# The gates' rows made on TensorE instead of through DRAM, column sums as one-column products, and a warm-up of three long products, in an adaLN block with linear attention

## The chip, the cores and the metric

One core of one Trainium2 chip. The metric is the device time of one execution of the program in microseconds (us); a lower one is better. The engines are called PE (TensorE, with PEld for its weight loads), DVE (VectorE), ACT (ScalarE), POOL (GpSimd) and SP (SyncE, which issues most transfers). Each engine works through its own instructions in the order in which the program has them, and waits on semaphores for the others.

## What is computed

A transformer block on x of 2048 tokens x 640 channels, with 32 heads of 20 channels. A vector c gives six modulation rows of 640 values; two of them, `ga` and `gb`, are the gates.

```python
mod = (_silu(c) @ w_mod).reshape(c.shape[0], 6, 1, -1)
sa, ca, ga, sb, cb, gb = (mod[:, 0], ..., mod[:, 5])
h = _layernorm(x) * (1 + ca) + sa
x = x + ga * A(h)          # linear attention, then @ wo
h = _layernorm(x) * (1 + cb) + sb
x = x + gb * B(h)          # relu(h @ w1 + b1)**2 @ w2 + b2
```

In the attention q and k go through a per-head matrix `w_phi` and two softmaxes each (of the product and of its negative); `kv` is the sum over tokens of phi_k times v, `z` the sum of phi_k, and the output is phi_q kv / (phi_q z + 1e-6). All inputs are float32.

## The kernel before

The weights of k and q are first folded with `w_phi` on TensorE (`fold`, L276). Then the 2048 tokens are worked in 16 tiles of 128. Nearly every large product is made of three: each operand is split into a high part (rounded to the fast float32r form by a ScalarE copy) and a low part (the rest, a VectorE subtraction, `lo`, L91 to L92), and high x high, high x low and low x high are added up in PSUM (`three`, `mm`).

The program has these stages. Up to about 60 us: warm-up products, the folds, the first tiles. From 60 to about 210 us: a loop over t = 2 to 13. In it TensorE's order is written by hand; the other engines' instructions are placed by a list scheduler, held only by some `issue_after` marks. Each turn makes the k, v and q products of a tile (`proj`, L82), and at even t the K/V sums of two tiles (`do_kv`, L453: 32 fp32 products a tile, each of two records, in four groups of 32 columns of the array), which gather in the PSUM bank `kvp[0]`. From 210 us a section ordered by hand on every engine but SP: the last tiles, the last K/V sums, the copy `kvs` of their bank to SBUF (ACT, L795), the row sums `z` spread over the partitions (`make_z`, PE L818, copied to `zb` by ACT L829 and DVE L827/L831), and then, tile by tile, the attention's output: DVE multiplies stored exponents by `zb` and sums them (L880, L882), makes the tails `ut` (L905) and the scaled exponents `ezb` (L916), which TensorE transposes (`tail` L932, `te` L950) and multiplies by K/V; then the product with `wo`. From about 376 us the MLP.

The modulation rows that are needed late (parts 2 to 5: `ga`, `sb`, `cb`, `gb`) are made beside this. For each part, DVE multiplies five row blocks of `w_mod` by the column `cs` = silu(c) and adds them up (`mac`, L290 and L292) into one tile of 128 x 640, called `wm` in the trace. What is still missing is the sum over the 128 partitions. Before the change it is made thus (`mod_turn` and `mod_sum`): PE transposes the tile in five blocks of 128 (L302; four after the K/V sums at t = 6, 8, 10 for parts 2, 3, 4, the fifth in the next turn's `t1`; all five in `kv_diags` for part 5), ACT copies the transposes to `mt` (L303), and DVE sums along the free axis (L307). That gives a column of five values on each partition. For parts 3 and 4 the column is what is wanted (`cols_b`, shift and scale of the second norm; 1 is added to the scale at t = 12). The gates are needed as a row on every partition: the column `gate_a` is written to DRAM, 4 bytes at a time, and read back to all partitions as `ga_b` (`spread_row`, SP L325 and L326, in t = 7). `ga_b` multiplies the rows of `wo` (`prep_wo`, from t = 9). The column `gate_b` is transposed on PE (L1284), copied by ACT (L1285), written to DRAM and read back as `gb_b` (SP L1286, L1287) when the attention ends; `gb_b` is used at the MLP's output.

The multiplies of part 5 (`gb_mac`) stand in the ordered section, the last two of them just before `biases`, the last two `do_kv` and the copy `kvs`.

The warm-up (L621, L623) is nine fp32 products of `ones` with `ones`, 128 x 128, and seven of 1 x 1; an fp32 product leaves two records.

Of the kernel before, what the change touches and what calls it, by code (L numbers as in the profile page):

```python
# [22 lines left out]
NC = D // P  # L23
# [8 lines left out]
CUT = ((0, 384), (384, D))  # L32
V_HEADS = ((0, 19), (19, H - 1))
EPS = 1e-5
POSTPONED = 4
WARM = 9
SHORT = 7
KEPT = NT - POSTPONED
W2_AT = 48
PLAIN = 2  # L40
# [15 lines left out]
def kernel(  # L56
# [23 lines left out]
    def mm(o, terms, first=True, last=True, skip=False):  # L80
        for i, (a, b) in enumerate(terms):
            nc.tensor.matmul(  # L82
                o, a, b,
                start=first and i == 0, stop=last and i == len(terms) - 1,
                skip_group_check=skip,
            )
# [4 lines left out]
    def lo(out_lo, full, hi, eng=None):  # L91
        (eng or nc.vector).tensor_tensor(out_lo, full, hi.bitcast(F32), op=ALU.subtract)  # L92
# [28 lines left out]
    def row(tag, name):  # L121
        return (pc if tag in ("s3", "s4") else mem).tile([P, D], F32, tag=tag, name=name, bufs=BUFS[tag])
# [19 lines left out]
    def tp(name):  # L142
        return psA.tile([P, 512], F32, tag="tp", name=name)
# [20 lines left out]
    ident = const.tile([P, P], F32, name="ident")  # L164
    make_identity(nc, ident)
    neg = const.tile([P, P], F32R, name="neg")
    plus = const.tile([P, 1], F32, name="plus")
    nc.gpsimd.memset(plus, 0.0)
    nc.gpsimd.memset(plus[32:64], 1.0)
# [90 lines left out]
    nc.vector.tensor_tensor(cs, c_t, ce, op=ALU.mult)  # L260

    nc.scalar.activation(neg, ident, AF.Copy, scale=-1.0)

    W = {}

# [25 lines left out]
        else:  # L291
            nc.vector.scalar_tensor_tensor(acc, t, cs[:, k : k + 1], prev, op0=ALU.mult, op1=ALU.add)  # L292

    MT = {}

    def mod_turn(part, p, *cs_):
        t = MT.setdefault(part, None) or row("s1", f"mt{part}")
        MT[part] = t
        a, n = cs_[0] * P, len(cs_) * P
        for i, c in enumerate(cs_):  # L300
            src = by_turn(MA[part])[:, c] if part in (3, 4) else MA[part][:, c * P : (c + 1) * P]
            nc.tensor.transpose(p[:, i * P : (i + 1) * P], src, ident)  # L302
        nc.scalar.activation(t[:, a : a + n], p[:, :n], AF.Copy)  # L303

    def mod_sum(part, dest):
        with tc.issue_after(newest(ET_.DVE)):
            nc.vector.tensor_reduce(dest, MT[part].rearrange("p (a b) -> p a b", b=P), axis=AX.X, op=ALU.add)  # L307

    def stage(col, k):
        t = row("s1", f"wm{col}_{k}")  # L310
# [11 lines left out]
    GD = [dram.tile([NC, P], F32, name=f"gate{h}") for h in range(2)]  # L322

    def spread_row(h, col, dest):
        nc.sync.dma_start(GD[h].rearrange("c p -> p c"), col)  # L325
        nc.sync.dma_start(dest, GD[h].rearrange("c p -> (c p)")[None, :].to_broadcast([P, D]))  # L326

    def ln_parts(xt, nm, spare=None):
        sm = small([P, 2], "sm", f"sm{nm}")
# [22 lines left out]
    def by_turn(ap):  # L352
        return ap.rearrange("p (f b) -> p b f", b=NC)
# [29 lines left out]
    def t1(j, *ds, more=None):  # L383
# [5 lines left out]
        if more:  # L389
            mod_turn(more[0], p[:, 256:], 4)  # L390
# [3 lines left out]
        if more:  # L394
            mod_sum(*more)

    def proj(nm, t, *between, cut=CUT):
        p = pj(f"p{nm}{t}")
# [60 lines left out]
    def do_q(t, *between):  # L459
        q_out(t, proj("q", t, *between))  # L460
# [42 lines left out]
    def biases():  # L503
        nc.sync.dma_start(bb, bass.AP(tensor=b2.tensor, offset=b2.offset, ap=[[0, P], [1, D]]))
# [7 lines left out]
    def gb_mac(n=1):  # L512
        for _ in range(n):
            k, t = GB.pop(0)
            mac(t, t, k, MA.get(5))
            MA[5] = t

    def wo_weights(*gs):
        for g in gs:
            prep_wo(g, ga_b)  # L520

    AFTER_KV = {
        6: lambda: mod_turn(2, tp("mc2"), 0, 1, 2, 3),
        8: lambda: mod_turn(3, tp("mc3"), 0, 1, 2, 3),
        10: lambda: mod_turn(4, tp("mc4"), 0, 1, 2, 3),
        12: lambda: t1(NT // 2 - 1, 2, 3),
    }
    gate_a = const.tile([P, NC], F32, name="gate_a")
    gate_b = const.tile([P, NC], F32, name="gate_b")
    gate_r = pc.tile([NC, P], F32, name="gate_r")  # L530
    LAST_COL = {7: (2, gate_a), 9: (3, cols_b[:, 0:5]), 11: (4, cols_b[:, 5:10])}
    SIDE = {
        2: lambda: mod_mac(2, 0, 1, 2),
        3: lambda: (mod_mac(2, 3, 4), mod_mac(3, 0)),
        4: lambda: mod_mac(3, 1, 2),
        5: lambda: (mod_mac(3, 3, 4), mod_mac(4, 0)),
        6: lambda: mod_mac(4, 1, 2),
        7: lambda: (spread_row(0, gate_a, ga_b), mod_mac(4, 3)),
        8: lambda: mod_mac(4, 4),
        9: lambda: wo_weights(0, 1),  # L540
        10: lambda: wo_weights(2),
        11: lambda: None,
        12: lambda: (nc.vector.tensor_scalar(cols_b[:, 5:10], cols_b[:, 5:10], 1.0, None, op0=ALU.add), wo_weights(3, 4)),
        13: lambda: gb_load(),
    }

# [71 lines left out]

    warm = tp("warm")
    for i in range(WARM):  # L620
        nc.tensor.matmul(warm[:, :P], ones, ones, start=True, stop=True)  # L621
    for i in range(SHORT):
        nc.tensor.matmul(warm[:1, :1], ones[:, :1], ones[:, :1], start=True, stop=True)  # L623
    for d in range(4):
        fold("k", d)()
    n0 = stats(XB[0], "a0")
# [84 lines left out]
    for t in range(2, NT - 2):  # L711
        j, i = divmod(t, 2)
        if i == 0 and j < NT // 2 - 2:
            load_x(j + 2)
        PK[t] = row("s2", f"k{t}")
        to_sb(proj("k", t), PK[t])
        if t == NT - 4:
            t1(j + 1, 0, 1)
        norm = j + 1 if i == 0 and t < NT - 4 else j + 2 if t == NT - 5 else None
        if norm:  # L720
            if not i:
                parts = ln_parts(XB[norm], f"a{norm}")
# [12 lines left out]
        spread(PK[t], EK[t], f"k{t}")  # L735
        exps(EK[t])
        if norm and not i:
            next(parts)
        if i and t < NT - 4:
            t1(j + 1, 2, 3)  # L740
        with tc.issue_after(newest(ET_.DVE)):
            k_norm(EK[t], t)
        if t < NT - POSTPONED:
            do_q(t, *([(1, 3, lambda: t1(j + 1, 4, more=LAST_COL.get(t)))] if i else []))
            if norm and i:
                with tc.issue_after(newest(ET_.Activation)), tc.issue_after(DONE[0]):
                    next(parts)
            if i:
                with tc.issue_after(DONE[1]):
                    q_chain(t)  # L750
            else:
                q_chain(t)
        if i == 0 and t < NT - 4:
            t1(j + 1, 0, 1)
        if t == NT - 6:
            parts = ln_parts(XB[j + 2], f"a{j + 2}")
            with tc.issue_after(newest(ET_.Activation)):
                next(parts)
        SIDE[t]()
# [28 lines left out]
    exps(EQ[q0])  # L788
    q_sums(q0)
    gb_mac(2)  # L790
    biases()
    do_kv(ka)
    do_kv(kb)
# [6 lines left out]
    def bank(nm):  # L800
        return psB.tile([P, 512], F32, tag="m", name=nm)
# [413 lines left out]
    for j in range(NB):  # L1215
# [16 lines left out]
            e_prod(b)  # L1232
        e_recip(b - 1)
        e_scale(b - 1)
        if j == 6:
            mod_sum(5, gate_b)
        load_e(b + 2)
        do_wo(j, 0, 0, *hooks(0, 0))
        if j - 1 in SPREAD:
# [559 lines left out]
```

## Time and profile before

| what | value |
|---|---|
| timed runs, median of 3 | 747.1 us (746.55 to 747.64) |
| the profiled execution's own time | 746.04 us |
| its span | 744.3 us |
| PE busy | 736.7 us (99%) |
| DVE busy | 599.0 us (80%) |
| ACT busy | 454.4 us (61%) |
| POOL busy | 168.1 us (23%) |
| granted clock, mean | 1.0 |

The profiled execution is one run, and its time is 1.74 us more than its span. In the rows of the profile, "L302 PE MATMUL mc<-ident,wm ... x4" is a group of four instructions of line 302 on PE that write `mc` and read `ident` and `wm`. A timeline's row begins with start and duration, and a bracket at its end gives the idle time of the engine before it and what ended that. A waits row gives total, number and longest wait.

### The profile page before, as it was taken

The numbers are of one execution on the slowest core, as the hardware profiler recorded it, in microseconds if no ns is written. First come the engines' busy times: TensorE is split into PE (matmuls) and PEld (weight loads), VectorE is DVE, ScalarE is ACT, GpSimd is POOL, SyncE is SP. The second block draws the span as 40 slices with busy tenths as digits, with TensorE's granted clock in tenths as the row PEclk, the third lists the DMA queues.
The fourth block names the chain that finished last, engine by engine and source line by source line (L and its number), as shares of the span: only waits on it lengthen the run. The fifth ranks groups of instructions, "written<-read, shape, count | busy, mean of one in ns | idle before, by whom it ended". The sixth has DMA issues, their size and how long they took to land.

```text
span 744.3 us, 16676 instructions
## 1 busy us (share of the span) xinstructions
PE 736.7 (99%) x6537; PEld 718.8 (97%) x6537; DVE 599.0 (80%) x1089; ACT 454.4 (61%) x1060; POOL 168.1 (23%) x352
## 2 busy tenths in 40 slices
PE   9999999999999999999999999999999999999997
PEld 9999999999999889998999999999999999999997
DVE  6598988978999999999655777877786776777766
ACT  5767666667863365567687667475573747647431
POOL 2001101001000347647303040231321313222110
PEclk9999999999999999999999999999999999999999
DMA  9912341343432354754885567897667768667461
GB/s 325 344 37 107 120 129 56 107 142 108 139 111 72 99 168 167 166 129 107 210 249 169 151 198 260 272 312 210 185 187 200 211 183 241 185 177 215 129 183 36
DMA packets 58801, 126.47 MB, mean 170 GB/s; under 512 B 7438, under 2 KB 16403, under 8 KB 58723
## 3 DMA queue, kind: packets, MB, share of 16 engines
q1 hardware_dynamic: 38636, 79.20, 32.6%
q0 software_dynamic: 17504, 40.90, 21.8%
q10 hardware_dynamic: 2583, 5.30, 1.9%
q8 instruction: 51, 0.84, 0.5%
q14 instruction: 27, 0.22, 0.1%
HBM read 100.74 MB, written 29.89 MB: 176 GB/s over the span
## 4 chain that ended last, share of the span: by engine, by line
PE 83%; DVE 10%; ACT 3%; issue 2%; POOL 1%; DMA 1%; ACTq 0%; DVEq 0%; POOLq 0%
PE up L82 25%; PE acc L82 18%; PE pwo L82 8%; PE pk L82 7%; PE pv L82 5%; PE acc3x L82 5%; PE pq L82 5%; PE te L950 2%; DVE dn L882 1%; DVE sk L444 1%; PE foldk L276 1%; PE numa L82 1%; DVE ek L436 1%; DVE ek L446 1%; DVE scr L880 1%
## 5 line engine op out<-in xcount | busy, mean ns | idle before, releaser
L82 PE MATMUL up<-h,w 128*128 128x256 f32 x1640 | 204.6, 276 | 0.1
L82 PEld LDWEIGHTS up<-h,w 128*128 128x128 f32 x1640 | 196.4, 188 | 0.7 <-DVE h L92 0.5
L1345 ACT ACTIVATE ft<-up,b_t 128x256 f32<-128x256 f32 x104 | 48.9, 471 | 95.7 <-PE up L82 95.3
L82 PE MATMUL acc<-w,ra 128*128 128x384 f32 x452 | 97.4, 335 | 0.0
L1346 DVE TENSOR_TENSOR ft<-ft 128x256 f32<-128x256 f32 x104 | 44.3, 426 | 42.9 <-ACT ft L1345 41.5
L82 PE MATMUL pwo<-wo,ot 128*128 128x384 f32 (+1 forms) x480 | 78.5, 314 | 0.0
L82 PE MATMUL pq<-wq,hT 128*128 128x384 f32 (+1 forms) x480 | 75.6, 312 | 0.0
L82 PEld LDWEIGHTS acc<-w,ra 128*128 128x128 f32 x452 | 72.7, 188 | 0.9 <-DVE ra L92 0.6
L82 PE MATMUL pk<-wk,hT 128*128 128x384 f32 (+1 forms) x480 | 73.1, 309 | 0.1
L82 PEld LDWEIGHTS pwo<-wo,ot 128*128 128x128 f32 x480 | 69.8, 188 | 2.8 <-issue 2.7
L82 PEld LDWEIGHTS pq<-wq,hT 128*128 128x128 f32 x480 | 71.1, 188 | 0.7 <-issue 0.5
L82 PE MATMUL pv<-wv,hT 128*128 128x384 f32 (+1 forms) x480 | 71.7, 307 | 0.0
L82 PEld LDWEIGHTS pk<-wk,hT 128*128 128x128 f32 x480 | 70.4, 188 | 1.0 <-DVE hT L92 0.5
L82 PEld LDWEIGHTS pv<-wv,hT 128*128 128x128 f32 x480 | 70.1, 188 | 0.0
L92 DVE TENSOR_TENSOR ra<-ft,ra 128x384 fp32r<-128x384 f32 (+2 forms) x86 | 36.8, 449 | 32.6 <-ACT ra L1369 18.8
L1455 POOL DMA_DIRECT2D ring_a<-td_a x34 | 18.5, 543 | 117.3 <-PE acc L82 106.3
L1369 ACT ACTIVATE ra<-ft 128x384 fp32r<-128x384 f32 x48 | 25.2, 526 | 28.4 <-DVE ft L1346 22.4
L82 PE MATMUL acc3x<-w,ra 128*128 128x256 f32 x231 | 39.5, 277 | 0.0
L82 PEld LDWEIGHTS acc3x<-w,ra 128*128 128x128 f32 x231 | 37.2, 188 | 0.0
L444 DVE TENSOR_REDUCE sk<-ek 128x64 f32<-128x1280 f32 x16 | 23.7, 1482 | 14.6 <-ACT ek L439 10.1
L1360 DVE TENSOR_TENSOR ft<-ft 128x128 f32<-128x128 f32 x136 | 33.4, 287 | 1.2
L335 POOL TENSOR_SCALAR sma<-sma 128x2 f32<-128x2 f32 x6 | 2.1, 343 | 133.7 <-ACT xb L334 133.7
(258 smaller groups left out, 1448.7 us busy)
## 6 DMA issues: line engine op xcount, KB each, us to landing
ring_c<-td_c POOLq DMA_DIRECT2D x34, 384.0 KB, 3.9
ring_a<-td_a POOLq DMA_DIRECT2D x34, 384.0 KB, 3.4
ring_b<-td_b POOLq DMA_DIRECT2D x34, 256.0 KB, 3.5
esp<-eq SPq DMA_DIRECT2D x12, 640.0 KB
el<-esp SPq DMA_DIRECT2D x12, 640.0 KB
rw<-in_w SPq DMA_DIRECT2D x23, 320.0 KB
wm<-in_w_mod SPq DMA_DIRECT2D x20, 320.0 KB
xb<-in_x SPq DMA_DIRECT2D x8, 640.0 KB
```

The lines of the kernel that those rows point to most:

```text
L82: nc.tensor.matmul(o, a, b, start=first and i == 0, stop=last and i == len(terms) - 1, skip_group_check=skip,)
L92: (eng or nc.vector).tensor_tensor(out_lo, full, hi.bitcast(F32), op=ALU.subtract)
L276: nc.tensor.matmul(p[g // 3][:, (g % 3) * 120 : (g % 3) * 120 + n], r, bd_t[:120, g * 120 : g * 120 + n], start=True, stop=True,)
L436: nc.vector.tensor_tensor(heads(e[:, s]), heads(t), over(mx[:, s]), op=ALU.subtract)
L444: nc.vector.tensor_reduce(s, heads(flat(e)), axis=AX.X, op=ALU.add)
L446: nc.vector.tensor_tensor(heads(flat(e)), heads(flat(e)), over(s), op=ALU.mult)
L950: nc.tensor.transpose(p[:124, a : a + P], EU[2 * j + i][:, 2 * g + c, :124], ident)
L1345: nc.scalar.activation(r, p, AF.Relu, bias=b1_t[:, f : f + 1])
L1346: nc.vector.tensor_tensor(r, r, r, op=ALU.mult)
L1360: nc.vector.tensor_tensor(t[:, o], t[:, a], t[:, b], op=op)
L1369: nc.scalar.activation(a[:, 0, :3], t[:, :3], AF.Copy)
L1455: nc.gpsimd.dma_start(RING[j, n, r], TD[n][r].bitcast(F32R))
```

## The change

It does four things.

1. Warm-up: three products of 128 x 384 columns (`ones` read three times) in place of nine of 128 and seven of one column.
2. Gates (parts 2 and 5): `gate_parts` splits the tile of 128 x 640 into a high part (ACT, L307 of the new kernel) and a low part (DVE, L91). `gate_row` multiplies a 128 x 128 matrix of ones (`ones_r`) by both, so that every partition of PSUM holds the sum over partitions, and ACT copies the row to `ga_b` or `gb_b` (L315). For part 2 the parts are made in t = 4 and the row at t = 6 in the place of the transposes (two products of 384 columns and two of 256); for part 5 the parts stand right behind the last two `gb_mac`, and the row is made in `kv_diags` (two products of 128 columns, two of 512). The DRAM tiles, their four transfers, the transpose L1284 and the copy L1285 are gone.
3. Parts 3 and 4: `mod_col` makes the column by 20 one-column fp32 products each (32 strided columns of the tile as the stationary operand, one column of ones moving, round four column groups), at t = 8 and 10 in the place of the transposes. ACT's copy adds the 1 to part 4. `mod_sum` is gone.
4. The fifth transposes of t = 7, 9, 11 (`more=`) are gone.

```diff
-WARM = 9
-SHORT = 7
+WARM = 3
...
+    nc.scalar.activation(ones_r, ones, AF.Copy)
...
-    def mod_turn(part, p, *cs_):
...
-    def mod_sum(part, dest):
...
+    def mod_col(part, dest):
+        m, p = by_turn(MA[part]), kvp[1]
+        for d in range(NC):
+            for c in range(0, P, 32):
+                nc.tensor.matmul(p[c : c + 32, d : d + 1], m[:, d, c : c + 32], ones[:, :1], start=(d == 0), stop=True, skip_group_check=True)
+        nc.scalar.activation(dest, p[:, :NC], AF.Identity, bias=ones[:, :1] if part == 4 else 0.0)
+
+    def gate_parts(part):
+        with tc.issue_after(newest(ET_.Activation)), tc.issue_after(newest(ET_.DVE)):
+            hi, low = GR_[part] = [row("s1", f"gate{part}_{i}").bitcast(F32R) for i in range(2)]
+            nc.scalar.activation(hi, MA[part], AF.Copy)
+            lo(low, MA[part], hi)
+
+    def gate_row(part, dest, *banks):
+        r = ones_r
+        for (a, b), p in banks:
+            mm(p, [(r, g[:, a:b]) for g in GR_[part]], skip=True)
+        for (a, b), p in banks:
+            nc.scalar.activation(dest[:, a:b], p, AF.Copy)
...
-    def spread_row(h, col, dest):
-        nc.sync.dma_start(GD[h].rearrange("c p -> p c"), col)
-        nc.sync.dma_start(dest, GD[h].rearrange("c p -> (c p)")[None, :].to_broadcast([P, D]))
...
-        6: lambda: mod_turn(2, tp("mc2"), 0, 1, 2, 3),
-        8: lambda: mod_turn(3, tp("mc3"), 0, 1, 2, 3),
-        10: lambda: mod_turn(4, tp("mc4"), 0, 1, 2, 3),
+        6: lambda: gate_row(2, ga_b, (CUT[0], kvp[1][:, :384]), (CUT[1], kvp[2][:, :256])),
+        8: lambda: mod_col(3, cols_b[:, 0:5]),
+        10: lambda: mod_col(4, cols_b[:, 5:10]),
...
-    LAST_COL = {7: (2, gate_a), 9: (3, cols_b[:, 0:5]), 11: (4, cols_b[:, 5:10])}
...
-        4: lambda: mod_mac(3, 1, 2),
+        4: lambda: (gate_parts(2), mod_mac(3, 1, 2)),
...
-        7: lambda: (spread_row(0, gate_a, ga_b), mod_mac(4, 3)),
+        7: lambda: mod_mac(4, 3),
...
     for i in range(WARM):
-        nc.tensor.matmul(warm[:, :P], ones, ones, start=True, stop=True)
-    for i in range(SHORT):
-        nc.tensor.matmul(warm[:1, :1], ones[:, :1], ones[:, :1], start=True, stop=True)
+        nc.tensor.matmul(warm[:, : 3 * P].rearrange("p (a n) -> p a n", a=3), ones, ones[:, None, :].to_broadcast([P, 3, P]), start=True, stop=True)
...
     gb_mac(2)
+    gate_parts(5)
     biases()
     do_kv(ka)
     do_kv(kb)
...
-        mod_turn(5, kvt[0][:, 3 * P :], 4)
-        mod_turn(5, bank("mc5"), 0, 1, 2, 3)
+        gate_row(5, gb_b, ((4 * P, D), kvt[0][:, 3 * P :]), ((0, 4 * P), bank("mc5")))
...
-            p = tp("gbt")[:NC, :P]
-            nc.tensor.transpose(p, gate_b, ident)
-            nc.scalar.activation(gate_r, p, AF.Copy)
-            nc.sync.dma_start(GD[1], gate_r)
-            nc.sync.dma_start(gb_b, GD[1].rearrange("c p -> (c p)")[None, :].to_broadcast([P, D]))
```

Two places show how the instructions now stand. The first is ACT at the end of the K/V sums (about 245 us before): `eq` are the exponents of tile 12, `wm_4` the finished tile of part 5, `gate_0` its high part, `kvs` the copy of the K/V bank, `zb` the copies of z. Before:

```order
L424 ACTIVATE vt_105<-pv_1_3324 128x16
L439 ACTIVATE eq_3083<-eq_3083 128x640
L440 ACTIVATE eq_3083<-eq_3083 128x640
L795 ACTIVATE kvs<-kvp_76 128x360
L829 ACTIVATE zb<-z_3450 128x3x60
L829 ACTIVATE zb<-z_3452 128x3x60
```

And in the changed kernel:

```order
L422 ACTIVATE vt_106<-pv_1_3329 128x16
L437 ACTIVATE eq_3088<-eq_3088 128x640
L438 ACTIVATE eq_3088<-eq_3088 128x640
L307 ACTIVATE gate_0_3369<-wm_4_3082 128x640
L790 ACTIVATE kvs<-kvp_76 128x360
L824 ACTIVATE zb<-z_3459 128x3x60
L824 ACTIVATE zb<-z_3461 128x3x60
```

A copy that needs the fifth multiply of part 5 now stands between the exponents and the copy `kvs`. On DVE that fifth multiply stands after the sum `rs_q` of the same exponents, and the low part behind it.

The second place is PE after the K/V sums at t = 8, where `mc` was the bank of part 3's transposes and `kvp_77` is the second K/V bank. Before:

```order
L82 MATMUL pv_1_2023<-wv_587,hT_1803 128x256 x3
L453 MATMUL kvp_76<-ek_1744,vt_104 21x2x20 x32
L453 MATMUL kvp_76<-ek_1894,vt_105 21x2x20 x32
L302 MATMUL mc_2118<-ident,wm_4_1580 128x128 x4
L82 MATMUL pq_0_2150<-wq_321,hT_1803 128x384 x3
```

And in the changed kernel:

```order
L81 MATMUL pv_1_2007<-wv_573,hT_1792 128x256 x3
L451 MATMUL kvp_76<-ek_1733,vt_105 21x2x20 x32
L451 MATMUL kvp_76<-ek_1883,vt_106 21x2x20 x32
L299 MATMUL kvp_77<-ones,wm_4_1570 32x1 x20
L81 MATMUL pq_0_2148<-wq_307,hT_1792 128x384 x3
```

Four transposes give way to 20 one-column products; what stands around them is the same. At t = 6 the four transposes give way to the gate row's four products in the same way.

More of the change, by code (lines that the diff above doesn't have):

```diff
@@ L166 @@
     neg = const.tile([P, P], F32R, name="neg")
+    ones_r = const.tile([P, P], F32R, name="ones_r")
     plus = const.tile([P, 1], F32, name="plus")
@@ L292, in mac @@
             nc.vector.scalar_tensor_tensor(acc, t, cs[:, k : k + 1], prev, op0=ALU.mult, op1=ALU.add)
-    MT = {}
-    def mod_turn(part, p, *cs_):
[L297 to L303, printed above, removed]
-    def mod_sum(part, dest):
-        with tc.issue_after(newest(ET_.DVE)):
-            nc.vector.tensor_reduce(dest, MT[part].rearrange("p (a b) -> p a b", b=P), axis=AX.X, op=ALU.add)
+    def mod_col(part, dest):
[4 more added lines that the diff above has]
+        nc.scalar.activation(dest, p[:, :NC], AF.Identity, bias=ones[:, :1] if part == 4 else 0.0)
+    GR_ = {}
+    def gate_parts(part):
[9 more added lines that the diff above has]
+            nc.scalar.activation(dest[:, a:b], p, AF.Copy)
     def stage(col, k):
@@ L320, in mod_mac @@
             MA[part] = t
-    GD = [dram.tile([NC, P], F32, name=f"gate{h}") for h in range(2)]
-    def spread_row(h, col, dest):
-        nc.sync.dma_start(GD[h].rearrange("c p -> p c"), col)
-        nc.sync.dma_start(dest, GD[h].rearrange("c p -> (c p)")[None, :].to_broadcast([P, D]))
     def ln_parts(xt, nm, spare=None):
@@ L381, with t1 @@
     DONE = []
-    def t1(j, *ds, more=None):
+    def t1(j, *ds):
         if 0 in ds:
@@ L388, in t1 @@
             t_in(XB[j], d, p[:, 256 * k : 256 * k + 256])
-        if more:
-            mod_turn(more[0], p[:, 256:], 4)
         for k, d in enumerate(ds):
@@ L393, in t1 @@
         DONE[:] = newest(ET_.Activation), newest(ET_.DVE)
-        if more:
-            mod_sum(*more)
     def proj(nm, t, *between, cut=CUT):
@@ L522 @@
     AFTER_KV = {
-        6: lambda: mod_turn(2, tp("mc2"), 0, 1, 2, 3),
-        8: lambda: mod_turn(3, tp("mc3"), 0, 1, 2, 3),
-        10: lambda: mod_turn(4, tp("mc4"), 0, 1, 2, 3),
+        6: lambda: gate_row(2, ga_b, (CUT[0], kvp[1][:, :384]), (CUT[1], kvp[2][:, :256])),
+        8: lambda: mod_col(3, cols_b[:, 0:5]),
+        10: lambda: mod_col(4, cols_b[:, 5:10]),
         12: lambda: t1(NT // 2 - 1, 2, 3),
     }
-    gate_a = const.tile([P, NC], F32, name="gate_a")
-    gate_b = const.tile([P, NC], F32, name="gate_b")
-    gate_r = pc.tile([NC, P], F32, name="gate_r")
-    LAST_COL = {7: (2, gate_a), 9: (3, cols_b[:, 0:5]), 11: (4, cols_b[:, 5:10])}
+    const.tile([P, 2 * NC], F32, name="fill3")
+    pc.tile([P, P], F32, name="gap4")
     SIDE = {
@@ L542 @@
         11: lambda: None,
-        12: lambda: (nc.vector.tensor_scalar(cols_b[:, 5:10], cols_b[:, 5:10], 1.0, None, op0=ALU.add), wo_weights(3, 4)),
+        12: lambda: wo_weights(3, 4),
         13: lambda: gb_load(),
@@ L743 @@
         if t < NT - POSTPONED:
-            do_q(t, *([(1, 3, lambda: t1(j + 1, 4, more=LAST_COL.get(t)))] if i else []))
+            do_q(t, *([(1, 3, lambda: t1(j + 1, 4))] if i else []))
             if norm and i:
@@ L1234 @@
         e_scale(b - 1)
-        if j == 6:
-            mod_sum(5, gate_b)
         load_e(b + 2)
```

## Prediction

> **What bounds the kernel now.** I read the page's busy times first, then TensorE's waits, then the timeline around each edit.
>
> ```profile
> span 744.3 us, 16676 instructions
> PE 736.7 (99%) x6537; PEld 718.8 (97%) x6537; DVE 599.0 (80%) x1089; ACT 454.4 (61%) x1060; POOL 168.1 (23%) x352
> ```
>
> TensorE (PE) is busy for 736.7 of 744.3 us, so an edit counts by the TensorE time that it removes or adds, or by a wait of TensorE that it makes or ends. The next view names TensorE's waits between 245 and 345 us, the attention stage.
>
> ```profile
> PE tail L932 <- DVE ut L905: 0.8, 2, 0.7
> PE tail L932 <- DVE ot L92: 0.6, 1, 0.6
> ```
>
> TensorE waits 1.4 us there, always for VectorE (DVE). How near VectorE is to its own limit is in the windows of 20 us (time, then busy time of PE, PEld, DVE, ACT, POOL):
>
> ```profile
> 245.00:265.00 20.00, 19.32 (x146) 17.60 (x147) 19.06 (x25) 8.26 (x23) 6.33 (x12) 1.00 0.51 159
> 325.00:345.00 20.00, 19.42 (x149) 17.79 (x148) 19.45 (x24) 13.93 (x33) 10.87 (x26) 1.00 0.52 141
> ```
>
> VectorE is busy for 19.06 and 19.45 of 20 us: in this stage both engines are nearly full, and a delay of either can reach the end. The granted clock is 1.00 in both.
>
> **Part 1, the warm-up.** TensorE's and VectorE's first rows (start, duration):
>
> ```profile
> 1.05 3.80 PE L621 MATMUL warm<-ones 128*128 128x128 f32 x18 [1.05 <-POOL bdc L159]
> 4.78 0.49 PE L623 MATMUL warm<-ones 128*1 128x1 f32 x14
> 5.20 1.04 PE L276 MATMUL foldk<-bd_t,raw_k 120*128 120x120 f32 x7
> 4.31 0.85 DVE L244 TENSOR_TENSOR bd_t<-bdc 120x360 f32<-120x360 f32 x2 [2.05 <-POOL mask L190]
> ```
>
> The new three products of 384 columns pass as many columns as nine of 128, so I let them end where the old nine end. The 14 short records between 4.78 and 5.20 fall away. The first fold then waits for the first of the two L244 instructions, which ends about half of 0.85 us after 4.31, with some overlap: 4.8 to 4.9. Gain 0.3 us; bounds 0 (a later load sets the folds) and 0.4.
>
> **Part 2, the column sums at t = 6, 8, 10.** Here are the K/V block and what follows it, without transposes (60 us), for part 2 (118 us) and part 4 (180 us).
>
> ```profile
> 60.37 1.48 PE L453 MATMUL kvp<-ek,vt 128*21 128x40 f32 x128
> 61.77 1.13 PE L82 MATMUL pq<-wq,hT 128*128 128x384 f32 x5
> ...
> 117.97 1.48 PE L453 MATMUL kvp<-ek,vt 128*21 128x40 f32 x128
> 119.38 0.66 PE L302 MATMUL mc<-ident,wm 128*128 128x128 f32 x4
> 119.79 1.48 PE L82 MATMUL pq<-wq,hT 128*128 128x384 f32 x7
> ...
> 178.83 1.48 PE L453 MATMUL kvp<-ek,vt 128*21 128x40 f32 x128
> 180.24 0.73 PE L302 MATMUL mc<-ident,wm 128*128 128x128 f32 x4
> 180.73 1.49 PE L82 MATMUL pq<-wq,hT 128*128 128x384 f32 x7
> ```
>
> From the block's start to the next product is 1.40 us without transposes, 1.82 and 1.90 with: four cost 0.42 and 0.50, and part 3 (rows below) 0.49. Together 1.41. The fifth transposes at t = 7, 9, 11, at a quarter of that each, add 0.36. What comes in their place has no row of its own, so it is priced by the nearest ones:
>
> ```profile
> L82 PE MATMUL pq<-wq,hT 128*128 128x384 f32 x167 | 32.3, 343 | 0.0
> L82 PE MATMUL pq<-wq,hT 128*128 128x256 f32 x165 | 22.1, 281 | 0.0
> L453 PE MATMUL kvp<-ek,vt 128*21 128x40 f32 x1024 | 12.6, 204 | 1.0 <-issue 0.9
> ```
>
> The gate's row at t = 6 is two products of 384 columns (32.3 / 167 = 0.193 us each) and two of 256 (0.134): 0.65. A column sum is 20 fp32 products, of two records each. Like the K/V products of L453 (12.6 / 1024 = 12.3 ns a record), they go round four column groups: 40 x 12.3 ns = 0.49 us, 0.98 for both. The other end is L623 above, 14 one-column records in one column group from 4.78 to 5.20, 30 ns each: 2.4 for both. I take 0.98, since L453 shares the column groups. Sum: -1.41 - 0.36 + 0.65 + 0.98 = -0.14.
>
> The Trainium skill, "TensorE: Matmul & The Clock Gate", section "Wait — 56ns, not 53.3ns?", says that start-to-start never falls below about 25 ns, however few columns pass. By that rule the 80 records would take 2.0 us and the sum would be 1.0 worse; L453's 12.3 ns speak against it.
>
> One more wait goes, that of the next transposes for ScalarE's (ACT's) copy of the sums:
>
> ```profile
> 124.72 0.66 PE L358 MATMUL ta<-ident,xb 128*128 128x128 f32 x4 [0.31 <-ACT mt L303]
> ```
>
> That is -0.3. The other copies, the VectorE sums of L307 and the gate's column turned at t = 7 of the output stage show in no wait of TensorE; I cost them, the two new VectorE subtractions of part 2 and the list scheduler's new order of loads and vector work before 210 us at nothing, 0.3 either way.
>
> **Part 3, the gate's write through DRAM.** The next rows are TensorE's and then SyncE's at t = 8, and after them the instruction queue's share of 16 DMA engines in 147 to 150.2 us and in 127 to 133 us.
>
> ```profile
> 147.87 1.50 PE L453 MATMUL kvp<-ek,vt 128*21 128x40 f32 x83
> 150.30 0.72 PE L453 MATMUL kvp<-ek,vt 128*21 128x40 f32 x45 [0.92 <-issue]
> 150.95 0.73 PE L302 MATMUL mc<-ident,wm 128*128 128x128 f32 x4
> 151.44 0.42 PE L82 MATMUL pq<-wq,hT 128*128 128x384 f32 x1
> ...
> 141.40 0.38 SPq L325 DMA_DIRECT2D gate<-gate_a  x1
> 150.25 0.34 SPq L326 DMA_DIRECT2D ga_b<-gate  x1
> ```
> ```profile
> q8 instruction: 1, 0.02, 6.1%
> ```
> ```profile
> q8 instruction: 1, 0.02, 0.9%
> ```
>
> This K/V block takes 150.95 - 147.87 = 3.08 us where another takes 1.41, and no semaphore is named. One instruction packet takes 6.1% of 16 x 3.2 = 3.1 us, against 0.9% of 16 x 6 = 0.9 in the other window. The gate's write of 4-byte values, issued at 141.40, is waited for until 150.25, just when TensorE goes on. I read it as an instruction fetch held up with that write. The change removes the write: -1.67 us. The other end is 0.
>
> The Trainium skill, "Runtime: NRT & Kernel Launch", section "Instruction fetch mechanics", says that crossing a 16 KiB block of instructions is mostly hidden. By that rule nothing comes back here and the time is 1.67 longer; this trace shows one crossing that is not hidden.
>
> **Part 4, the second gate's parts ahead of the K/V copy.** In the new order ScalarE's copy `gate_0` (L307) stands just before the copy `kvs`, and it needs the fifth multiply of the gate (L292). The rows before, ScalarE, VectorE and TensorE:
>
> ```profile
> 244.73 0.72 ACT L440 ACTIVATE eq<-eq 128x640 f32<-128x640 f32 x1
> 245.35 0.46 ACT L795 ACTIVATE kvs<-kvp 128x360 f32<-128x360 f32 x1
> 247.37 0.86 ACT L829 ACTIVATE zb<-z 128x180 f32<-128x180 f32 x4 [1.56 <-PE z L818]
> ...
> 246.88 1.80 DVE L292 SCALAR_TENSOR_TENSOR wm<-wm,cs,wm 128x640 f32<-128x640 f32 x2
> 249.44 0.28 DVE L827 COPY zb<-z 128x120 f32<-128x120 f32 x1
> 249.75 1.49 DVE L880 TENSOR_TENSOR scr<-el,zb 128x1280 f32<-128x1280 f32 x1
> ...
> 246.46 0.87 PE L818 MATMUL z<-kvs,ident 21*128 21x360 f32 x8
> ```
>
> The multiplies end at 248.68. A copy of 128x640, priced by the exponent's 0.72, ends at 249.4; `kvs`, 0.46 more, at 249.85. TensorE's z products, which ran at 246.46, wait on `kvs`: 3.4 us late, with the whole in-order queue of TensorE behind them. VectorE's side: ScalarE copied z from 0.91 us after z's start to 1.77 after it, so now until 251.6, and VectorE's last copy of z (0.28) lets L880 start at about 252.0 instead of 249.75: 2.25 late. The new subtraction on VectorE, priced by a multiply's 0.9, starts at 249.4 and lies inside that wait.
>
> Behind it stands the gate's row, in the place of five transposes:
>
> ```profile
> 253.04 0.27 PE L302 MATMUL kvt<-ident,wm 128*128 128x128 f32 x1
> 253.51 0.72 PE L82 MATMUL pq<-wq,hT 128*128 128x256 f32 x4
> L982 PE MATMUL numa<-ot,neg 128*128 128x512 f32 x2 | 0.9, 447 | 0.0
> ```
>
> The five took 0.47. Two products of 128 columns (0.11 each, as the transposes) and two of 512 (0.26 by the 384-column row's rate, 0.45 by L982) make 0.74 to 1.12: +0.3, bounds 0.2 and 0.65.
>
> So TensorE comes 3.4 + 0.3 = 3.7 late, and gives back the 1.4 that it used to wait for VectorE: 2.3 remain. VectorE is 2.25 late and full, so it cannot give much back, and where it paced TensorE (340 us) that is the same 2.3. Taken: +2.3; bounds 2.0 and 3.0.
>
> **Sum.** -0.3 - 0.14 - 0.3 - 1.67 + 2.3 = -0.1 us. The profiled execution took 746.04 us (span 744.3 and 1.74 around it), so it would take 745.9. The three timed runs of before have a median 1.06 above it, 747.1; on their scale I predict 747.0: gains before 160 us that the wait at 246 us takes back.
>
> **The rivals.**
>
> *The late fetch is not the gate's doing* (slower, 14%). For it: the row names only "issue", and timed and profiled runs differ by 1.06 us, so the profile may hold an accident. Against it: both ended together. If any fetch may come late in the dense K/V block, nothing is gained: 748.7. It decides once less than 0.2 of the 1.67 comes back.
>
> *Column products at 30 ns a record* (11%). For it: L623's rate, and strided weights. Against: L453. 1.4 more: 748.4.
>
> *The long warm-up does not open the clock in time* (8%). The clock is then low while the folds run; the old loop's records took 3.80 / 18 = 0.21 us, the old folds' 1.04 / 7 = 0.15, and if a stretch as long as the warm-up's 3.8 us ran at half speed, 1.9 would be lost, less what loads hide: about 1.7 more, 748.7. Against it: the same columns in the same time.
>
> *The timed runs hold more of the late fetch than the profiled one* (faster, 22%). Their surplus of 1.06 us would then go too: 745.9, and between 744.9 and 746.4 with the bounds of the other terms. For it: only a cause outside the profiled run explains the surplus. Against it: nothing shows where it lies.
>
> *The change does not do what it says*: the z wait would fail to appear only if ScalarE reached `gate_0` with the multiplies long done; they end 3.3 us after `kvs` started before, so I give this no chance of its own.
>
> **How the numbers follow.** 45% stay with the forecast, 747.0, whose own range is 746.0 to 748.4 (column products dear at the top; z's delay 2.0 and the gains at their best below). About 0.2%, 1.5 us, is what a measurement of this kernel tells from no change: faster means under 745.6, slower over 748.6. Of the forecast's 45%, 9 are faster, 31 the same, 5 slower; of the fetch rival's 14%, 9 slower and 5 the same; of the column rival's 11%, 7 the same and 4 slower; of the clock's 8%, 6 slower and 2 the same; of the surplus's 22%, 15 faster and 7 the same. Sums: 0.24, 0.52, 0.24. The range that leaves out 2 in 10 is 744.8 to 749.2.
>
> **What would show it.** In the changed kernel's profile: first fold near 4.9; no wait of `ta` for ScalarE at 124; K/V block at t = 8 of 1.4 us and no instruction packet of 3 us; column sums of 0.5 us each; a wait of TensorE of about 3.4 us at z, released by `kvs`, and none for VectorE at the next tail. A z wait under 2 us, or TensorE's waits for VectorE still there after it, would make part 4 wrong; a K/V block still at 3 us, part 3.

## The result, and the profile after

The changed kernel takes 754.53 us (median of 4, 752.78 to 755.70), the kernel before beside it 747.37. The ratio is 1.0085, with a 95% interval of 1.0064 to 1.0106: slower by about 6.4 us (the two medians are 7.2 apart), where no change was forecast and 749.2 was the range's upper end. The profiled execution took 752.78 us, 6.74 more than that of before. One timed run below, of the kernel with the column sums apart, took 1227 us at a mean granted clock of 0.558 and is left out of its ratio.

The page's first lines, and TensorE's longest waits in the changed kernel:

```profile
span 751.1 us, 16752 instructions
PE 739.1 (98%) x6578; PEld 719.6 (96%) x6578; DVE 598.4 (80%) x1086; ACT 454.5 (61%) x1060; POOL 171.9 (23%) x352
...
PE z L813 <- ACT kvs L790: 3.1, 1, 3.1
PE kvp L299 <- issue: 2.2, 1, 2.2
...
PE acc L81 <- DMA ring_b<-td_b: 0.6, 1, 0.6
PE tail L926 <- POOL rn L1150: 0.4, 1, 0.4
```

The span grew by 6.8 us and TensorE's busy time by 2.4, so 4.4 of the loss is time in which TensorE stands still. Two long waits are new: one for `kvs` ahead of z, one named only "issue" in the column products. The waits for VectorE at the tails are gone; one of 0.4 us for GpSimd (`rn`) came there, and one of 0.6 us for a transfer in the MLP.

Around z, the rows of ScalarE, TensorE and VectorE in the changed kernel, and last TensorE's rows before the change (z itself, at 246.46, is shown above):

```profile
249.13 0.74 ACT L307 ACTIVATE gate<-wm 128x640 fp32r<-128x640 f32 x1 [3.27 <-DVE wm L293]
249.77 0.45 ACT L790 ACTIVATE kvs<-kvp 128x360 f32<-128x360 f32 x1
...
245.28 1.85 PE L81 MATMUL pq<-wq,hT 128*128 128x384 f32 x9
250.28 1.57 PE L813 MATMUL z<-kvs,ident 21*128 21x360 f32 x8 [3.14 <-ACT kvs L790]
251.77 7.95 PE L81 MATMUL pq<-wq,hT 128*128 128x384 f32 x36
259.56 0.49 PE L835 MATMUL kvt<-ident,kvs 128*120 128x128 f32 x3
260.58 1.64 PE L81 MATMUL pq<-wq,hT 128*128 128x256 f32 x13
...
253.39 1.49 DVE L874 TENSOR_TENSOR scr<-el,zb 128x1280 f32<-128x1280 f32 x1
```
```profile
244.71 1.82 PE L82 MATMUL pq<-wq,hT 128*128 128x384 f32 x9
...
247.27 5.61 PE L82 MATMUL pq<-wq,hT 128*128 128x384 f32 x36
252.72 0.49 PE L840 MATMUL kvt<-ident,kvs 128*120 128x128 f32 x3
```

ScalarE waits 3.27 us for the fifth multiply, copies the gate's high part, and only then `kvs`. From the first q product to z it is 5.00 us here and 1.75 before: 3.25 more, as the prediction had it (3.4). But then the 36 q products from z's end to the turned K/V take 259.56 - 251.77 = 7.79 us, where before they took 252.72 - 247.27 = 5.45. The windows of 2 us say why (time, the window's length, PE busy, then PEclk, the granted clock, and at the end DMA share and GB/s; 0.79 is the mean of a window in which the clock changed):

```profile
248.00:250.00 2.00, 0.00 (x0) 1.00 0.35 93
250.00:252.00 2.00, 1.73 (x9) 0.50 0.80 239
252.00:254.00 2.00, 2.00 (x7) 0.50 0.54 159
254.00:256.00 2.00, 2.00 (x12) 0.50 0.00 0
256.00:258.00 2.00, 2.00 (x13) 0.79 0.00 0
258.00:260.00 2.00, 2.00 (x15) 1.00 0.00 0
```

After the wait TensorE's granted clock is 0.50 until about 256.8 us. That costs 2.34 us in the q products and 0.68 in z itself (1.49 from z to the next product, 0.81 before), 3.0 in all.

The mean granted clock of each timed run shows that such stretches differ from run to run. At half clock for 3.4 us, a run of 750 us has a mean lower by 0.002. The changed kernel's four runs have 0.992 to 0.995; the profiled one is the quickest of them and has the 0.995, so the profile shows less half clock than the median run holds. Of 35 runs of the kernel before beside the first experiments, 24 have 0.997 or 0.998 and a median of 749.47 us, 11 have 0.999 or 1.000 and 747.61 us. So the kernel before, too, loses 1.9 us in part of its runs, and its profile, with a clock of 1.00, is one of the others. No profile shows where the clock falls in these runs.

The second new wait is at t = 8; t = 10, with the same products, has none.

```profile
147.62 1.44 PE L451 MATMUL kvp<-ek,vt 128*21 128x40 f32 x126
148.92 0.74 PE L299 MATMUL kvp<-ones,wm 128*32 128x1 f32 x37
151.85 0.22 PE L299 MATMUL kvp<-ones,wm 128*32 128x1 f32 x1 [2.19 <-issue]
```
```profile
179.28 1.44 PE L451 MATMUL kvp<-ek,vt 128*21 128x40 f32 x126
181.25 0.97 PE L81 MATMUL pq<-wq,hT 128*128 128x384 f32 x4
```

The smaller steps of the change, the first fold behind the warm-up, the gate's row at t = 6 and the next transposes:

```profile
4.87 7.13 PE L277 MATMUL foldk<-bd_t,raw_k 120*128 120x120 f32 x60
...
119.75 0.86 PE L81 MATMUL kvp<-gate,ones_r 128*128 128x384 f32 x4
120.44 0.86 PE L81 MATMUL pq<-wq,hT 128*128 128x384 f32 x4
...
124.75 0.60 PE L360 MATMUL ta<-ident,xb 128*128 128x128 f32 x4
```

### The profile page after: what moved, and what is told of

Same layout as the page of the kernel before. It is cut to its first block, busy times and chain, and to the rows that moved or that the text cites. A ratio compares the mean times of both kernels' runs of the same rounds, so it can differ in the third digit from the quotient of the medians.

```text
span 751.1 us, 16752 instructions
## 1 busy us (share of the span) xinstructions
PE 739.1 (98%) x6578; PEld 719.6 (96%) x6578; DVE 598.4 (80%) x1086; ACT 454.5 (61%) x1060; POOL 171.9 (23%) x352
## 4 chain that ended last, share of the span: by engine, by line
PE 88%; DVE 4%; ACT 3%; issue 2%; DMA 2%; POOL 1%; SPq 0%; ACTq 0%; DVEq 0%; POOLq 0%
PE up L81 24%; PE acc L81 17%; PE pwo L81 9%; PE pq L81 8%; PE pk L81 8%; PE pv L81 7%; PE acc3x L81 5%; PE te L944 2%; PE numa L81 1%; PE kvp L451 1%; DMA ring_b<-td_b 1%; PE numb L81 1%; PE foldk L277 1%; PE foldq L277 1%; PE ta L360 1%
## 5 line engine op out<-in xcount | busy, mean ns | idle before, releaser
L81 PE MATMUL pq<-wq,hT 128*128 128x384 f32 (+1 forms) x480 | 77.8, 318 | 0.0
L81 PEld LDWEIGHTS pq<-wq,hT 128*128 128x128 f32 x480 | 73.5, 194 | 1.4 <-issue 1.0
L91 DVE TENSOR_TENSOR ra<-ft,ra 128x384 fp32r<-128x384 f32 (+2 forms) x86 | 36.8, 449 | 32.6 <-ACT ra L1356 19.4
```

Source lines behind the costliest of these rows:

```text
L81: nc.tensor.matmul(o, a, b, start=first and i == 0, stop=last and i == len(terms) - 1, skip_group_check=skip,)
```

## The experiments

The theory after the result: the loss is the wait of TensorE for `kvs` and the half clock behind it, and a wait that belongs to a dense stretch of instructions took the place of the one that the DRAM write had made. Each ratio is to the kernel before, timed beside it: its median was 749.22 us beside the first four runs below (late parts to the write alone), 748.77 beside the plain row and the two runs built on it, and 748.09 beside the last three.

**The parts made later.**

```diff
-    def gate_parts(part):
+    def gate_parts(part, eng=None):
...
-            lo(low, MA[part], hi)
+            lo(low, MA[part], hi, eng)
...
     gb_mac(2)
-    gate_parts(5)
...
+        gate_parts(5, nc.gpsimd)
```

The last line stands at the end of `make_z`, behind the copies of z.

> The changed kernel with the second gate's parts made behind the copies of z (ScalarE's copy after them, the subtraction on GpSimd), nothing else moved. Theory (the wait of TensorE for the K/V copy, and a clock that falls to half behind it, make the loss): z runs at its old place, the granted clock is 1.00 from 246 to 262 us, the K/V rows to the tail take as long as in the kernel before; 3.2 us of wait and 3.0 us of half clock go, 1.05 us of waiting for VectorE comes back: 754.5 - 5.2 = 749.3, or 748.5 if the wait for a ring at 507 us goes too. Rival (the clock falls for another reason, such as the phase of the power control or the long gate products): only wait less the wait for VectorE, 754.5 - 2.2 = 752.3, with a clock of 0.5 still to be seen.

Measured: 749.99 us, ratio 1.0017 (1.0002 to 1.0033). Against the changed kernel's 1.0085 that is 5.1 us less, as the theory said. TensorE at z, then VectorE's first product with z and GpSimd's subtraction:

```profile
249.41 0.88 PE L812 MATMUL z<-kvs,ident 21*128 21x360 f32 x8
250.21 5.64 PE L81 MATMUL pq<-wq,hT 128*128 128x384 f32 x36
255.69 0.49 PE L835 MATMUL kvt<-ident,kvs 128*120 128x128 f32 x3
...
252.51 2.76 DVE L874 TENSOR_TENSOR scr<-el,zb 128x1280 f32<-128x1280 f32 x1
...
252.35 1.57 POOL L91 TENSOR_TENSOR gate<-wm,gate 128x640 fp32r<-128x640 f32 x1 [5.52 <-ACT gate L307]
```

z follows without a wait and the q products take 5.48 us, as before. Something new: VectorE's product takes 2.76 us beside GpSimd's subtraction, while the median of the twelve such products in this run is 1.49, and the next tail waits 1.7 us for VectorE. The wait at t = 8 stays (2.3 us), and here the clock falls behind that one too:

```profile
154.00:156.00 2.00, 2.00 (x8) 0.50 0.42 132
```

**The wait kept, the idle time filled.**

```diff
     def make_z():
+        fill = tp("fillz")
+        mm(fill[:, :384], [(ones_r, W["q", 0][:, 0, :384])] * 17)
```

> The changed kernel with 17 products of 384 columns, whose result nobody reads, ahead of the z products, so that TensorE works through most of the wait for the K/V copy. Theory: the wait for the copy stays (z still 3.2 us late) but the clock stays at 1.00 behind it: the products from 250 to 260 us take 3.0 us less, 751.5. Rival (the fall of the clock is not due to TensorE's idle time): clock 0.5 still seen, 754.5.

Measured: 751.06 us, ratio 1.0022 (1.0008 to 1.0036). The time is within 0.5 us of the 751.5 that was expected. The ratio is lower than 751.5 to the 747.37 of the result, 1.0055, since the kernel before took 749.22 here, with 24 of its 35 runs at a mean clock under 0.999. The mechanism is in the trace:

```profile
247.09 1.85 PE L81 MATMUL pq<-wq,hT 128*128 128x384 f32 x9
248.78 3.17 PE L81 MATMUL fillz<-wq,ones_r 128*128 128x384 f32 x17
252.06 0.88 PE L815 MATMUL z<-kvs,ident 21*128 21x360 f32 x8
252.87 5.75 PE L81 MATMUL pq<-wq,hT 128*128 128x384 f32 x36
258.45 0.49 PE L837 MATMUL kvt<-ident,kvs 128*120 128x128 f32 x3
...
252.00:254.00 2.00, 1.94 (x14) 1.00 0.85 224
```

z is as late as in the changed kernel (4.97 us after the first q product), the clock stays 1.00, and the q products take 5.58 us instead of 7.79. So the clock fell because TensorE idled, not because of what ran behind the wait. The timed runs agree: nine of ten have a mean clock of 0.998 to 1.000, where the changed kernel's four have 0.992 to 0.995. At t = 8 this run waits 2.2 us, with a half clock behind it.

**The second gate alone.** The kernel before with `gate_parts(5)` behind `gb_mac(2)` and `gate_row(5, ...)` in `kv_diags`, without `mod_sum(5, ...)` and the turn through DRAM at the end.

```diff
...
     gb_mac(2)
+    gate_parts(5)
...
-        mod_turn(5, kvt[0][:, 3 * P :], 4)
-        mod_turn(5, bank("mc5"), 0, 1, 2, 3)
+        gate_row(5, gb_b, ((4 * P, D), kvt[0][:, 3 * P :]), ((0, 4 * P), bank("mc5")))
```

> The kernel before with the second gate alone made the new way (its parts ahead of the K/V copy, its row by products of ones); warm-up, first gate and the columns as before. Theory: the whole loss is here: wait 3.2, half clock 3.0, gate row 0.25, less 1.05 of waiting for VectorE: 747.4 + 5.4 = 752.8. Rival (other parts lose too): under 751.

Measured: 752.68 us, ratio 1.0060 (1.0039 to 1.0080), 4.5 us slower; 5.4 were expected. The ten runs spread from 751.06, the profiled one with a mean clock of 0.998, to 758.88 with 0.991. TensorE's waits, and the clock behind z:

```profile
PE z L834 <- ACT kvs L811: 3.1, 1, 3.1
PE kvp L470 <- issue: 1.5, 2, 1.0
...
252.00:254.00 2.00, 2.00 (x11) 0.57 0.74 227
254.00:256.00 2.00, 2.00 (x11) 0.58 0.17 65
256.00:258.00 2.00, 2.00 (x16) 1.00 0.00 0
```

The same wait, but the low clock lasts 3.4 us here (1.72 + 1.68, at half clock), against more than 6 in the changed kernel, and the q products behind z take 7.05 us, 1.6 more than at full clock. The part alone gives about two thirds of the loss. The wait for instructions in the K/V sums of t = 8 is the old one: this kernel still has the write of 4-byte values.

**The write through DRAM alone.** The kernel before; the first gate's column is turned on TensorE and written in rows of 512 bytes.

```diff
-        7: lambda: (spread_row(0, gate_a, ga_b), mod_mac(4, 3)),
+        7: lambda: mod_mac(4, 3),
...
+        if t == 8:
+            pg = tp("gat")[:NC, :P]
+            nc.tensor.transpose(pg, gate_a, ident)
+            nc.scalar.activation(gate_r, pg, AF.Copy)
+            nc.sync.dma_start(GD[0], gate_r)
+            nc.sync.dma_start(ga_b, GD[0].rearrange("c p -> (c p)")[None, :].to_broadcast([P, D]))
```

> The kernel before with the first gate's column turned on TensorE and written to DRAM in five rows of 512 bytes instead of 640 values of 4 bytes; all else as before. Theory of the prediction (the instruction fetch is held up by the 4-byte write): the K/V block at t = 8 takes 1.4 us instead of 3.08, no instruction packet of 3 us, 747.4 - 1.6 = 745.8. Rival (the fetch comes late wherever a dense stretch of TensorE's instructions meets a block's end): the block still takes 2.5 to 3.5 us or another one does, 747.4 within 0.5.

Measured: 745.26 us, ratio 0.9960 (0.9943 to 0.9978). The K/V block at t = 8, and the queues from 146 to 150.2 us:

```profile
148.11 1.48 PE L453 MATMUL kvp<-ek,vt 128*21 128x40 f32 x128
149.52 0.73 PE L302 MATMUL mc<-ident,wm 128*128 128x128 f32 x4
...
q1 hardware_dynamic: 289, 0.98, 70.6%
q8 instruction: 1, 0.02, 1.4%
```

The block takes 1.41 us and the instruction packet 1.4% of 16 x 4.2 = 0.94 us, although data transfers take 70.6% of the engines at that time. In the kernel before, the write's packets end at 142.8 us, nothing else moves from then on, and yet the instruction packet that starts at 147.21 takes 3.1 us, and the read-back behind the write is issued only at 150.25. So it was not busy queues that made this packet long; it went with the write. Other causes exist: a packet of the changed kernel took 2.6 us at 267.8 us, with no such write and 71.5% of the engines' time in use, and TensorE did not wait there.

In time the gain is 3.0 us, more than the 1.67 of the profile. None of the 34 runs without the write (this kernel, its repetition and the run with the long warm-up) has a mean clock under 0.999, and 24 of 35 runs of the kernel before have one. An estimate from these runs, 24/35 of the 1.9 us between the two groups, is 1.3 us, which makes up the difference. Timed once more:

> The kernel before without the 4-byte write, timed once more beside the next two: 0.996 of the kernel before, within 0.15%.

Measured: 745.03 us, ratio 0.9967 (0.9954 to 0.9981). The profiled execution here is one of two in 12 (four of 10 above) that took 747.4 to 748.3 us, about 3 us more than the others. Its K/V block at t = 8 takes 1.41 us again; its longest wait is that of the transposes for ScalarE's copy of the sums, which the changed kernel does not have:

```profile
PE ta L358 <- ACT mt L303: 2.4, 3, 1.6
```

**A plain fp32 row.** The changed kernel without parts for the second gate.

```diff
-    gate_parts(5)
...
-        gate_row(5, gb_b, ((4 * P, D), kvt[0][:, 3 * P :]), ((0, 4 * P), bank("mc5")))
+        own_ = ((4 * P, D), kvt[0][:, 3 * P :]), ((0, 4 * P), bank("mc5"))
+        for (a, b), p in own_:
+            mm(p, [(ones, MA[5][:, a:b])], skip=True)
+        for (a, b), p in own_:
+            nc.scalar.activation(gb_b[:, a:b], p, AF.Copy)
```

> The changed kernel with the second gate's row made by fp32 products of ones with the finished tile itself, in the same place behind the turned K/V, so that no high and low parts are made: nothing stands before the K/V copy on ScalarE and nothing is subtracted beside VectorE. Theory (wait for the K/V copy and the half clock behind it are the loss, and in the run with late parts GpSimd's subtraction slowed VectorE by 1.3 us): z at its old place with clock 1.00, VectorE's first product with z at 1.5 us again, the gate row at most 0.6 longer than the five transposes, but the wait of 2.2 us in the column products at t = 8 still there, with or without half a clock behind it: 1.0005 to 1.0025 of the kernel before. Rival (more is lost behind the attention stage): over 1.004.

Measured: 749.19 us, ratio 1.0011 (0.9999 to 1.0023), within what was expected. No wait at z; the wait at t = 8 is still there, at the same record:

```profile
152.84 0.22 PE L299 MATMUL kvp<-ones,wm 128*32 128x1 f32 x1 [2.19 <-issue]
```

**The column sums apart from the K/V sums.** The plain-row kernel, with `mod_col` behind the ninth q product of t = 8 and 10 (the long line is shortened here).

```diff
-        8: lambda: mod_col(3, cols_b[:, 0:5]),
-        10: lambda: mod_col(4, cols_b[:, 5:10]),
...
-            do_q(t, ...)
+            do_q(t, ... [(0, 9, lambda: mod_col(3 if t == 8 else 4, ...))] if t in (8, 10) else [])
```

> The kernel of the run before this one with the two column sums moved from right behind the K/V sums to the middle of the q products of the same turn. Theory A (the wait of 2.2 us at t = 8 comes because 256 K/V records and 80 column records follow each other at about 10 ns each, faster than the next block of instructions comes): no wait over 0.5 us at t = 8, 2.2 to 3.7 us less than the run before this one, 0.996 to 0.998 of the kernel before. Theory B (the block's instructions come late there whatever stands in it, since transfers fill the queues then): a wait of 1 to 3 us stays at t = 8, in the K/V sums or behind them, and the time stays within 0.1% of the run before this one.

Measured: 746.82 us, ratio 0.9975 (0.9964 to 0.9985). The wait shrinks to half a microsecond:

```profile
151.07 0.66 PE L299 MATMUL kvp<-ones,wm 128*32 128x1 f32 x30
152.22 0.39 PE L299 MATMUL kvp<-ones,wm 128*32 128x1 f32 x10 [0.49 <-issue]
```

**The blocks' ends moved.** The plain-row kernel with 32 one-column products more in the warm-up.

```diff
+    for i in range(32):
+        nc.tensor.matmul(warm[:1, :1], ones[:, :1], ones[:, :1], start=True, stop=True)
     for d in range(4):
```

> The kernel with the plain fp32 row and 32 one-column products (128 records, 0.8 to 1.6 us) more in the warm-up, so that every block of 256 instructions of TensorE ends elsewhere in the program. Theory A with the block's end deciding: the wait behind 39 of 40 column records at t = 8 goes or moves to another record, perhaps to another turn. Theory B or a wait that belongs to that instruction: 2.2 us at the same record.

Measured: 746.64 us in one run (plain row: 747.89 to 751.25 in 12), although the first fold starts 1.74 us later than in the plain-row kernel's profile (6.86 against 5.12). The wait is gone:

```profile
150.65 0.74 PE L299 MATMUL kvp<-ones,wm 128*32 128x1 f32 x38
151.32 2.92 PE L81 MATMUL pq<-wq,hT 128*128 128x384 f32 x15
```

Nothing was changed at t = 8, only how many instructions stand before it. So the wait belongs to a place in the stream of instructions, and the traces say which. In the five profiles that have it (changed kernel, late parts, fill, plain row, sums apart) it stands behind the 1616th product of TensorE, although in the run with the sums apart that is the 30th column record and not the 39th. In each, the only instruction packet between 140 us and the end of the wait takes 0.93 to 1.05 us and ends 1.36 to 1.44 us before TensorE goes on, and the wait ends 4.23 to 4.34 us after the K/V sums began. Setting the sums apart did not bring the instructions sooner: nine q products fill 1.79 us of the time, and the wait is 1.70 shorter. In the shifted run the packets start at 143.84 and 151.26 us, with none in the K/V sums. That TensorE waits there for the instructions of that packet (theory A, a block's end) is the reading of these figures; no row names the engine that a packet is for.

**The warm-up alone.** The kernel without the 4-byte write, with the long warm-up.

```diff
-WARM = 9
-SHORT = 7
+WARM = 3
...
```

> That kernel with the long warm-up (three products of 384 columns) in place of the old one; the rest the same, TensorE's instructions 52 fewer ahead of the folds. Theory of the prediction: the first fold starts 0.3 us earlier, of which the loads of the next weights take back a part: 0 to 0.3 us less than the run before this one. Rival (the moved ends of the instruction blocks decide): a wait named only issue of 0.5 us or more appears at some K/V block, and the time is above the run before this one.

Measured: 744.82 us, ratio 0.9959 (0.9948 to 0.9970), against 0.9967 with the old warm-up: no difference that the intervals can tell. The wait named issue that the rival had does not appear. It has the lowest median of all, 3.1 us under the kernel before.

**The sums apart, with the old warm-up.** The kernel with the sums apart, and in it:

```diff
-WARM = 3
+WARM = 9
+SHORT = 7
...
```

> The kernel with the plain fp32 row and the column sums in the middle of the q products, with the old warm-up: 52 instructions more ahead of everything on TensorE, so that the block that ended within the column records at t = 8 (a wait of 0.49 us) ends among sparse products. Theory (dense stretch and block's end): no wait at t = 8, 0.2 to 0.7 us under the same kernel with the long warm-up, that is 0.9965 to 0.9975 of the kernel before, the best of the changed kernels. Rival: the wait stays or moves to another K/V block, 0.9975 or more.

Measured: 747.59 us, ratio 0.9998 (0.9988 to 1.0009): the expected gain did not come. The rival's number came, but not its wait: none named issue is left, at t = 8 or elsewhere. At 199 us, in t = 11, transposes wait for a copy of ScalarE:

```profile
PE ta L361 <- ACT hfa L372: 1.1, 1, 1.1
```

What moved that copy is open: nothing was written there, but ScalarE's and VectorE's order before 210 us is the list scheduler's. Nor is it shown that this wait cost the gain: the profiles of the two kernels with the sums apart have the same span, 746.3 us, one with the wait of 0.49 us and one with this.

## Why the prediction was wrong

The two profiles' spans differ by 6.8 us. By TensorE's places:

| step | predicted | measured |
|---|---|---|
| up to the q product behind the last K/V sums (244.71 before, 245.28 after) | -2.4 | +0.57 |
| wait for `kvs` ahead of z | +3.4 | +3.25 |
| half clock behind it | not seen | +3.0 |
| gate's row for five transposes | +0.3 | +0.23 |
| given back from there to 348 us (the waits at the tails fall from 1.4 to 0.4) | -1.4 | -1.6 |
| the rest, behind 348 us | 0 | +1.4 |

**Part 4 failed in its price.** The step was "TensorE comes 3.4 + 0.3 = 3.7 late, and gives back the 1.4". The order, the waiting instruction, the wait and what was given back came out; the step priced the work behind the wait at the full clock, and at half clock it took 3.0 us more. The fill run shows the clock's part: with the same wait and no idle TensorE, the products behind it take 5.58 us instead of 7.79. The granted clock of 1.00 that I quoted belonged to stretches in which TensorE never idled for more than 0.7 us at a time, and the change made it idle for 3.1. The median of the timed runs is 1.75 us above the profiled one; the mean clocks, 0.992 and 0.993 in the other three against 0.995, leave room for that (an estimate: 0.002 of 753 us, at half clock, is 1.5 us).

The Trainium skill, "TensorE: Matmul & The Clock Gate", section "What's actually happening", has the clock fall to half after an idle window of about 3.4 us. The idle time of 3.14 us here is shorter, but near enough that the page should have made me price it. And idle times of 2.2 us at t = 8 also brought 0.50 in three runs (parts later, fill, plain row) and not in the changed kernel's own profile, so a full window of idle time is not needed.

**Part 3 was right about the write and wrong about the change.** "I read it as an instruction fetch held up with that write" is shown by the run without the 4-byte write, and by the run with the second gate alone, which keeps the write and has a packet of 2.9 us and the wait. "The change removes the write: -1.67 us" failed: the 80 instructions of a column sum (40 products and their weight loads) behind the 256 of the K/V sums made a longer dense stretch, and a wait of 2.19 us came at its end. Density alone does not make it: the same stretch at t = 10 has no wait, and 128 instructions more ahead of it end the one at t = 8. The rival of the late fetch named this place, and I gave it 14%, with the wrong alternative: it is not that the write was innocent, both causes exist. The rival on timed runs, that they hold more of the late fetch than the profiled run, fits the gain of 3.0 us without the write, and the mean clocks say what the surplus is: half clock in 24 of 35 runs of the kernel before, worth about 1.3 us by the estimate above.

**Part 2 was about right.** The gate's row at t = 6 took 0.69 us (0.65 predicted). The column sum at t = 10 took 181.25 - 179.28 - 1.40 = 0.57 us (0.49). The wait of `ta` for ScalarE is gone.

The Trainium skill's floor of about 25 ns from start to start ("TensorE: Matmul & The Clock Gate", section "Wait — 56ns, not 53.3ns?") would make 1.0 us of a column sum (an estimate: 40 records); the trace disagrees, with 0.57.

**Part 1 came out in this profile and was worth nothing.** The first fold starts 0.33 us earlier; by the q folds 0.09 is left, and alone the long warm-up is within the intervals of the old one. (In the runs with the plain row and with the long warm-up alone the first fold starts at 5.12 and 5.21 us, so even these 0.33 us do not come in every run.)

**The MLP** (the rest of the table) was costed at nothing. It has 0.6 us of waiting for a ring's transfer in the changed kernel and in the runs with late parts and the plain row (0.4), and none in the fill run. Whether it follows from the change or from where the start happens to fall is open.

## What to carry to other kernels

Price a new wait of TensorE twice: once for the idle time, and once for the products behind it at half clock, 1.6 and 3.0 us here behind a wait of 3.1 us; behind the waits of 2.2 us the clock fell in three profiles of four. Before moving a step up an in-order queue, look for the copy behind it that TensorE needs next, and put the step behind that copy. Keep stretches of very short TensorE instructions short and apart, since adding to one can make the instruction supply the bound, and any edit earlier in the program then moves the effect.

## What the runs showed of the hardware

- The granted clock reads 1.00 or 0.50 in these traces; other values are means of windows in which it changed. A fall to 0.50 lasted 3.4 us behind one wait of 3.1 us (second gate alone) and 6.8 us behind another of the same length (changed kernel).
- An instruction packet of 16 KB took 2.9 and 3.1 us while a write of 640 values of 4 bytes to DRAM was open (second gate alone, kernel before), with no other packet moving, and 0.9 to 1.9 elsewhere, also with 70% of the transfer engines' time in use; one of the changed kernel took 2.6.
- TensorE ran dry for 2.2 us after about 330 instructions in a row at some 10 to 15 ns a matrix product (0.5 us with nine longer products between), in five profiles behind the 1616th product of the program and 1.4 us after an instruction packet had landed, and not when 128 instructions more stood ahead of them.
- A VectorE product of 128 x 1280 took 2.76 us instead of 1.49 while GpSimd subtracted two tiles of 128 x 640.
